# All 32 turning transfers issued by SyncE in a two-spectrum filter kernel

## The chip, the core and the metric

The kernel runs on one core of a Trainium2 chip. The core has five engines with queues of their own: TensorE (PE in the profile; PEld is its weight load), VectorE (DVE), ScalarE (ACT), GpSimd (POOL) and SyncE (SP). Sixteen DMA engines move data between memory and the on-chip buffer, and inside that buffer. A DMA is issued by one of the queues; the queue then goes on to its next instruction, and a semaphore tells of the landing.

The metric is the device time of one execution in microseconds, the median over several runs. All times below are in microseconds.

## The reference

One input x of 2048 rows by 1024 columns (bf16) goes through two spectral filters, A and B, and a gate mixes the two results row by row:

```python
X = jnp.fft.rfft2(x.astype(jnp.float32), axes=(-2, -1))
a = jnp.fft.irfft2(X * (A_w_r + 1j * A_w_i), s=(2048, 1024), axes=(-2, -1)).astype(jnp.bfloat16)
b = jnp.fft.irfft2(X * (B_w_r + 1j * B_w_i), s=(2048, 1024), axes=(-2, -1)).astype(jnp.bfloat16)
g = sigmoid((x * gate_w).sum(-1, keepdims=True))
return g * a + (1 - g) * b
```

The weights have 2048 rows by 513 columns. Both filters read the same x, so the forward transform is made once and the inverse transform twice.

## The kernel before

**How the work is tiled.** The 2048 rows are split as 128 times 16: a row is 16 times a partition number plus a remainder n2 from 0 to 15. Every transform is written as matrix products against constant matrices. The forward part goes through the rows in pairs of n2 (stage S1), then through the columns (stage D), then through the 16 remainders (stage S2). The spectrum lies in 16 slots on 128 partitions, in four groups `sq` of four slots.

**The products with the weights.** VectorE multiplies each pair of slots with the weights of A (b = 0) and of B (b = 1): `prod`, tiles of 128 x 2052.

**The inverse over the 16 remainders, and the turn.** `stage_iw` (for b = 0) and `stage_i1` (for b = 1) multiply the products with a small constant matrix on TensorE and leave two results of 128 x 1024 each, for j = 0 and 1, the two halves of the partitions. ScalarE or VectorE evicts each result from PSUM into a tile V in RING. There are seven such tiles (`"v": ("ring", 14)`, two cells each), used again and again. Then one DMA per tile, 256 KB, moves it from RING into TV so that partitions and remainders change places: this is the turning transfer, `dma("turn" ...)` or `dma("turnw" ...)`.

- A wide turn (`turnw`, from `stage_iw`, all 16 for b = 0) writes 8 partitions of TV, 16 rows of 1024 elements (2 KB) in each. Its access pattern is 8x16x1024.
- An ordinary turn (`turn`, from `stage_i1`, all 16 for b = 1) writes 16 partitions, 8 rows of 2 KB in each: 16x8x1024. It belongs to one half `th` of the remainders: th = 0 for n2 below 8, th = 1 for the others.

So there are 32 turns, 8 MB in all. In this text "(1,3,0) j=0" is the ordinary turn of b = 1, sq = 3, th = 0, first half of the partitions.

**The inverse over the rows, the columns, the folds.** For each remainder n2, stage S1 inverse multiplies turned data with the gated matrices FM (for A) and RM (for B). For n2 = 0 to 3 it is cut into an A part (`S1A`) and a B part (`S1B`); for the others it is one group (`S1H`). `S1A` needs all 16 wide turns. `S1B` and `S1H` need the ordinary turns of their half th as well. The result is evicted (G), multiplied with the constant DI (`Di2`, `Di`), evicted again (o), and folded by VectorE (u, e, y0, y1) into a row tile y, which SyncE stores (`dma("out" ...)`). The fold's tiles u and y lie in RING too, in cells which the V tiles used before.

**What sets the order.** The whole order is written out. `ORDER` is a table with the sequence of all nodes, `ENGS` gives the engine of each node where the node allows several (p TensorE, a ScalarE, d VectorE, g GpSimd, s SyncE), and `CELLS` gives each tile its place. `Plan.replay` reads the three, and `Sched` turns data dependences into semaphore waits. Every engine executes its nodes strictly in the order of the table. A DMA waits in its queue for what it needs, and what stands behind it in the same queue waits with it.

**The two queues of interest.** SyncE (SP) issues the loads of x, the constants F, DM, SK, RM and DI, eight ordinary turns and the nine stores. GpSimd (POOL) issues 44 weight loads, the 16 wide turns and eight ordinary ones (24 turns). The constant DI is read first by `Di2`. In the program it is loaded by

```python
cload("sp", DI, 0, "DI", 0, 2048, ["DI"], more=wk[1])
```

which waits for the weights of B (`more=wk[1]`), and its place among the turns is set by `ORDER`. All DMAs are issued by one line of the helper, L426 in the profile; evictions by ScalarE are L417, by VectorE L418, VectorE's two-operand instructions L395, matrix products L392.

## Time and profile before

| what | value |
|---|---|
| median of 3 runs | 123.09 (122.49 to 123.79) |
| profiled execution, its own time | 124.25 |
| its span, first to last instruction of the program | 122.4 |
| mean granted TensorE clock | 0.979 |
| busy: PE / DVE / ACT / POOL | 103.8 / 103.4 / 93.5 / 40.1 |
| turns issued by POOL / by SP | 24 / 8 |
| one turn's issue on POOL, mean; TV<-RING, issue to landing on POOL / SP, median | 0.577; 5.7 / 7.8 |
| DMA traffic, mean over the span | 228 GB/s |

How to read it: the span is cut into 40 slices of 3.06 each on the profile's page, and a digit is the busy share in tenths. The chain of waits is followed back from the last instruction. Durations of matrix products overlap, since the array is pipelined. An instruction's "idle before" is the time for which its engine had nothing to do ahead of it, with the releaser that the profile infers; where the named releaser had long been done or is not what the instruction reads, it was another, often a DMA.

The turns run from 51.6 on. Until 77 VectorE multiplies without a pause; then the last evictions and turns of b = 1 follow, and from 85.7 on the inverse over the rows.

### The profile page before, as it was taken

How to read it: one execution, taken by the hardware profiler on the slowest of the kernel's cores; microseconds unless marked ns; L12 is line 12 of the kernel's file. 1: busy time of each engine (PE TensorE's matmuls, PEld its weight loads, DVE VectorE, ACT ScalarE, POOL GpSimd, SP SyncE). 2: the span in 40 equal slices, each digit the busy share in tenths (PEclk: the TensorE clock that was granted, in tenths of full speed). 3: DMA queues.
4: the chain of work that ended last, by engine and by line, in shares of the span. 5: the costliest groups of instructions: out<-in, count | busy, mean ns of one | idle time of the engine just before them, and what ended most of it. 6: DMA issues, size and time to landing. Idle time of an engine off the chain costs nothing.

```text
span 122.4 us, 3773 instructions
## 1 busy us (share of the span) xinstructions
PE 103.8 (85%) x1652; PEld 71.6 (58%) x1652; DVE 103.4 (84%) x139; ACT 93.5 (76%) x106; POOL 40.1 (33%) x72
## 2 busy tenths in 40 slices
PE   6879968999999998999797977795999999993820
PEld 2258747797665753454254424342899999992500
DVE  0459999928889999999999999759586599999990
ACT  4098999277799789999798897623499999984930
POOL 0006599999994000163525323031500000000000
PEclk9999999999999999999999999999999999999587
DMA  4999999999999960047886677699999102148664
GB/s 81 395 422 414 402 354 251 329 348 318 334 284 343 314 171 3 5 99 169 227 215 182 174 196 220 174 244 247 269 262 237 44 5 102 70 193 327 253 261 171
DMA packets 10754, 27.86 MB, mean 228 GB/s; under 512 B 4049, under 2 KB 4049, under 8 KB 10482
## 3 DMA queue, kind: packets, MB, share of 16 engines
q0 software_dynamic: 6272, 14.73, 42.9%
q1 hardware_dynamic: 4320, 12.88, 30.6%
q8 instruction: 13, 0.21, 0.7%
q10 hardware_dynamic: 146, 0.02, 0.1%
q14 instruction: 3, 0.02, 0.1%
HBM read 15.01 MB, written 4.19 MB: 157 GB/s over the span
## 4 chain that ended last, share of the span: by engine, by line
DVE 54%; PE 21%; ACT 11%; issue 5%; DMA 5%; SPq 1%; DVEq 0%
DVE WAB L395 23%; PE PS L392 21%; DVE RING L395 14%; DVE TV L395 5%; DMA WAB<-in_A_x_dram 5%; ACT R L417 4%; DVE RING L418 4%; DVE R L395 4%; ACT RING L417 3%; ACT TV L417 3%; DVE TV L418 2%; DVE FM L395 1%; DVE WAB L418 1%; DVE R L418 1%; ACT WAB L417 1%
## 5 line engine op out<-in xcount | busy, mean ns | idle before, releaser
L417 ACT ACTIVATE RING<-PS 128x1024 bf16<-128x1024 f32 x38 | 37.0, 1023 | 13.4 <-PE PS L392 12.9
L395 DVE TENSOR_TENSOR RING<-WAB 128x1024 bf16<-128x1024 bf16 (+1 forms) x42 | 23.6, 612 | 7.6 <-DMA WAB<-in_A_x_dram 5.1
L426 POOL DMA_DIRECT2D TV<-RING x24 | 13.8, 577 | 36.0 <-ACT RING L417 31.4
L395 DVE TENSOR_TENSOR WAB<-R,WAB 128x2052 bf16<-128x2052 bf16 x20 | 23.8, 1226 | 0.1
L417 ACT ACTIVATE WAB<-PS 128x1024 bf16<-128x1024 f32 (+1 forms) x25 | 20.2, 970 | 2.7 <-DVE WAB L395 2.1
L392 PE MATMUL PS<-WAB,SK 64*32 64x512 bf16 (+1 forms) x512 | 20.5, 377 | 1.6 <-DVE RING L418 0.6
L417 ACT ACTIVATE R<-PS 128x1024 bf16<-128x1024 f32 (+1 forms) x20 | 17.6, 947 | 2.2 <-PE PS L392 2.2
L418 DVE CAST RING<-PS 128x1024 bf16<-128x1024 f32 x10 | 12.1, 1220 | 4.6 <-PE PS L392 4.6
L392 PEld LDWEIGHTS PS<-WAB,SK 64*32 64x32 bf16 (+1 forms) x512 | 9.4, 95 | 10.3 <-DVE WAB L395 2.0
L392 PE MATMUL PS<-DM,TV 128*128 128x256 bf16 x128 | 15.2, 274 | 0.1
L392 PE MATMUL PS<-FM,TV 128*128 128x128 bf16 x128 | 13.3, 220 | 2.2 <-ACT WAB L417 2.1
L392 PE MATMUL PS<-TV,RING 128*128 128x256 bf16 (+1 forms) x128 | 12.6, 253 | 2.8 <-DVE RING L395 1.4
L392 PEld LDWEIGHTS PS<-DM,TV 128*128 128x128 bf16 x128 | 13.5, 114 | 2.3 <-issue 1.0
L392 PEld LDWEIGHTS PS<-FM,TV 128*128 128x128 bf16 x128 | 12.5, 113 | 3.1 <-ACT WAB L417 2.4
L417 ACT ACTIVATE TV<-PS 128x1024 bf16<-128x1024 f32 x14 | 13.3, 1043 | 0.5 <-PE PS L392 0.5
L392 PEld LDWEIGHTS PS<-TV,RING 128*128 128x128 bf16 x128 | 10.2, 98 | 5.2 <-DVE RING L395 1.9
L392 PE MATMUL PS<-RM,TV 128*128 128x128 bf16 x128 | 13.1, 219 | 0.0
L392 PEld LDWEIGHTS PS<-RM,TV 128*128 128x128 bf16 x128 | 12.6, 114 | 0.0
L426 POOL DMA_DIRECT2D WAB<-in_A_w_r_dram x11 | 6.7, 612 | 11.4 <-DMA WAB<-in_A_x_dram 11.4
L392 PE MATMUL PS<-RING,SK 64*64 64x511 bf16 (+2 forms) x160 | 9.3, 340 | 0.8 <-ACT R L417 0.5
L395 DVE TENSOR_TENSOR TV<-R,WAB 128x2052 bf16<-128x2052 bf16 x8 | 9.6, 1226 | 0.4 <-DVE R L418 0.4
L392 PE MATMUL PS<-TV,SK 64*64 64x512 bf16 x128 | 8.5, 380 | 1.3 <-DVE WAB L395 0.9
(46 smaller groups left out, 117.2 us busy)
## 6 DMA issues: line engine op xcount, KB each, us to landing
TV<-RING POOLq DMA_DIRECT2D x24, 256.0 KB, 5.7
WAB<-in_A_x_dram SPq DMA_DIRECT2D x8, 512.0 KB, 7.8
out_dram<-RING SPq DMA_DIRECT2D x7, 512.0 KB, 2.9
TV<-RING SPq DMA_DIRECT2D x8, 256.0 KB, 7.8
WAB<-in_A_w_r_dram POOLq DMA_DIRECT2D x2, 513.0 KB, 8.8
WAB<-in_A_w_i_dram POOLq DMA_DIRECT2D x2, 513.0 KB, 8.1
WAB<-in_B_w_r_dram POOLq DMA_DIRECT2D x2, 513.0 KB, 7.7
WAB<-in_B_w_i_dram POOLq DMA_DIRECT2D x2, 513.0 KB, 9.9
```

What stands on the lines that cost most here:

```text
L392: return lambda e: e.matmul(o, l, r, start=start, stop=stop, skip_group_check=True)
L395: return lambda e: e.tensor_tensor(out=o, in0=a, in1=b, op=op)
L417: return [lambda e: e.activation(o, i, ACT.Copy)]
L418: return [lambda e: e.tensor_copy(o, i)]
L426: n = P.add(name, es, lambda e: [lambda q, d=d, s=s: q.dma_start(d, s) for d, s in pairs()], reads, writes, dma=kind, **kw)
```

## The change

All 32 turns are issued by SyncE. GpSimd keeps the weight loads and issues nothing after them. The table of order, the engines of all other nodes, and all places of tiles are the same. In the code two arguments change, and 24 letters g of `ENGS` become s:

```diff
 ENGS = (
...
-    "ppaddddddpaapaappppdaaddddappaapppppadpdpdddaappdaadppgggggggggggaapaaaasdddddpddaapaapddddddddddddddddddaappaagpaaggggg"
-    "gggggppaapaapaappaapppapaaddppgggggggppaddadpppdadpaddssssggggggsssssppppppppapdappddaapapapapapappppaaadddddddddddddppa"
+    "ppaddddddpaapaappppdaaddddappaapppppadpdpdddaappdaadppgggggggggggaapaaaasdddddpddaapaapddddddddddddddddddaappaaspaasssss"
+    "sssssppaapaapaappaapppapaaddppsssssssppaddadpppdadpaddsssssssssssssssppppppppapdappddaapapapapapappppaaadddddddddddddppa"
...
-            dma("turn", ("sp", "pool")[j], lambda j=j: [(AP(TV, (64 * j + sq) * pt + vat(b, 8 * th), [[4 * pt, 16], [(2048, 1024)[b], 8], [1, 1024]]),
+            dma("turn", "sp", lambda j=j: [(AP(TV, (64 * j + sq) * pt + vat(b, 8 * th), [[4 * pt, 16], [(2048, 1024)[b], 8], [1, 1024]]),
...
-            dma("turnw", "pool", lambda j=j: [(AP(TV, (64 * j + 32 * a + sq) * pt + b * 16384, [[4 * pt, 8], [1024, 16], [1, 1024]]),
+            dma("turnw", "sp", lambda j=j: [(AP(TV, (64 * j + 32 * a + sq) * pt + b * 16384, [[4 * pt, 8], [1024, 16], [1, 1024]]),
```

TensorE's, VectorE's and ScalarE's queues hold the same instructions in the same order as before. GpSimd's queue ends after the last weight load. What changes is SyncE's queue. Its beginning, from the last constants of the forward part on, was this before (RM is the matrix for B in the inverse over the rows; s_act and s_dve are the semaphores of ScalarE and VectorE, s_d and a number that of a DMA; xN counts equal rows in sequence):

```order
L426 DMA SK<-c_SK 128x1152
L426 DMA RM<-c_RM 128x2048 [waits s_d17,s_d18,s_d16,s_d19,s_d15,s_d20,s_d14,s_d21,s_d13,s_d22,s_d23]
L426 DMA TV<-RING 16x8x1024 [waits s_act]
L426 DMA TV<-RING 16x8x1024 x2
L426 DMA TV<-RING 16x8x1024 [waits s_act]
```

and it is this now:

```order
L426 DMA SK<-c_SK 128x1152
L426 DMA RM<-c_RM 128x2048 [waits s_d17,s_d18,s_d16,s_d19,s_d15,s_d20,s_d14,s_d21,s_d13,s_d22,s_d23]
L426 DMA TV<-RING 8x16x1024 [waits s_act] x7
L426 DMA TV<-RING 8x16x1024
L426 DMA TV<-RING 8x16x1024 [waits s_act]
L426 DMA TV<-RING 16x8x1024 [waits s_act]
L426 DMA TV<-RING 8x16x1024 [waits s_act]
L426 DMA TV<-RING 8x16x1024 x2
```

The wide turns (8x16x1024) now stand on SyncE's queue, behind RM, and each waits there for its own eviction. The second place is around the load of DI. Before, SyncE's queue had, behind the first four ordinary turns:

```order
L426 DMA TV<-RING 16x8x1024 [waits s_act]
L426 DMA DI<-c_DI 128x2048
L426 DMA TV<-RING 16x8x1024
L426 DMA TV<-RING 16x8x1024 [waits s_dve]
L426 DMA TV<-RING 16x8x1024 [waits s_act]
L426 DMA TV<-RING 16x8x1024 [waits s_dve]
```

and now, from the last wide turn on:

```order
L426 DMA TV<-RING 8x16x1024
L426 DMA TV<-RING 16x8x1024 [waits s_act]
L426 DMA TV<-RING 16x8x1024 x2
L426 DMA TV<-RING 16x8x1024 [waits s_act]
L426 DMA TV<-RING 16x8x1024
L426 DMA TV<-RING 16x8x1024 [waits s_dve] x3
L426 DMA TV<-RING 16x8x1024
L426 DMA TV<-RING 16x8x1024 [waits s_act]
L426 DMA DI<-c_DI 128x2048
L426 DMA TV<-RING 16x8x1024 x3
L426 DMA TV<-RING 16x8x1024 [waits s_dve]
```

Six turns that were GpSimd's now stand ahead of DI: (1,2,0) j=1, (1,3,0) j=1, and the four turns j=1 of th = 1, namely (1,0,1), (1,3,1), (1,1,1) and (1,2,1). The last of these waits for the last eviction but one of the whole stage. The four turns j=0 of th = 1 stay behind DI.

## The prediction

> **What bounds the kernel now.** I read the chain of waits first, from 84 us on, because the edit touches nothing before 51 and the turns' readers stand here.

> ```profile
> 83.86 1.98 PE PS L392 x64
> ...
> 86.94 5.57 PE PS L392 x80
> ...
> 92.53 1.02 ACT WAB L417
> 93.55 2.76 ACT R L417 x3
> 96.31 0.03 issue
> 96.34 0.76 DVE RING L395 x2
> ```

> Up to 92.5 TensorE carries it, after 96.3 VectorE, to the end. The timelines of PE and of VectorE show the two hand-overs:

> ```profile
> 85.72 2.30 PE L392 MATMUL PS<-FM,TV 128*128 128x128 bf16 x32
> 87.86 1.95 PE L392 MATMUL PS<-RM,TV 128*128 128x128 bf16 x32
> 89.69 2.80 PE L392 MATMUL PS<-DI,R 128*128 128x128 bf16 x32
> ```

> ```profile
> 93.19 0.76 DVE L395 TENSOR_TENSOR RING<-WAB 128x512 bf16<-128x512 bf16 x2
> 96.34 0.76 DVE L395 TENSOR_TENSOR RING<-WAB 128x512 bf16<-128x512 bf16 x2 [2.38 <-ACT R L417]
> ...
> 100.63 1.22 DVE L418 CAST WAB<-PS 128x1024 bf16<-128x1024 f32 x1
> ```

> S1A, S1B and Di2 of n2 = 0 to 3 follow each other on PE without a gap; the third group reads DI. VectorE stands idle for 2.38 ahead of the fold u of n2 = 0. The releaser named writes R, which this fold doesn't read. It reads o of n2 = 0, evicted by ScalarE at 93.55, and writes a RING tile that a V tile had: that of (1,1,1) j=1. Its turn's issue and its landing:

> ```profile
> 85.83 1.04 POOL L426 DMA_DIRECT2D TV<-RING  x2 [1.21 <-DVE RING L418]
> 87.17 0.53 POOL L426 DMA_DIRECT2D TV<-RING  x1 [0.29 <-ACT RING L417]
> ```

> ```profile
> TV<-RING POOLq DMA_DIRECT2D x1, 256.0 KB, 9.9
> ```

> The second of the pair starts at about 86.35 and lands 9.9 later, at 96.24, just ahead of 96.34. So VectorE's last stretch waits for the backlog of turns. From 77 to 97 that backlog keeps the DMA engines full (share 0.90), and two stages before they are not:

> ```profile
> 52.90:54.20 1.30, 1.30 (x28) 0.58 (x16) 1.30 (x2) 1.30 (x2) 0.74 (x2) 1.00 0.46 66
> 57.00:66.00 9.00, 7.46 (x192) 3.34 (x188) 8.97 (x9) 8.04 (x10) 3.58 (x7) 1.00 0.85 224
> 77.00:97.00 20.00, 17.88 (x414) 13.84 (x399) 13.41 (x17) 12.38 (x14) 3.17 (x6) 1.00 0.90 224
> ```

> (The last two columns are the DMA engines' share and GB/s.)

> **The change part by part.** *The issue itself.* GpSimd starts a turn 0.29 after the eviction (row 87.17: ScalarE's eviction ended at 86.88). SyncE needs 0.02:

> ```profile
> 76.12 1.03 ACT L417 ACTIVATE RING<-PS 128x1024 bf16<-128x1024 f32 x1
> ```

> ```profile
> 77.17 0.62 SPq L426 DMA_DIRECT2D TV<-RING  x1
> ```

> An issue takes 0.62 there against 0.53 to 0.60. Each turn is thus issued 0.27 sooner, if SP isn't held by a turn ahead; nothing that ends late reads that, so I cost it at nothing.

> *DI moves back.* This is the term that counts. SP's own timeline before:

> ```profile
> 77.17 3.67 SPq L426 DMA_DIRECT2D TV<-RING  x4
> 80.88 1.08 SPq L426 DMA_DIRECT2D DI<-c_DI  x1
> 82.01 5.63 SPq L426 DMA_DIRECT2D TV<-RING  x4
> ```

> ```profile
> DI<-c_DI SPq DMA_DIRECT2D x1, 512.0 KB, 8.7
> ```

> DI landed at 80.88 + 8.7 = 89.55, and Di2 began at 89.69: already no slack. Now SP must first issue (1,2,1) j=1, whose eviction on ScalarE ends at

> ```profile
> 85.86 1.02 ACT L417 ACTIVATE RING<-PS 128x1024 bf16<-128x1024 f32 x1 [2.26 <-PE PS L392]
> ```

> 86.88. With 0.02, the issue of 0.62 and 0.04 between two, DI is issued at 87.56, 6.7 later. Behind it in the queue wait the four turns j=0 of th = 1 (issued from 82.01 on before); ahead of it, in the DMA engines, what SP issued before. For their pace I take the landing of the turn at 77.17, which finds its queue empty (the second row is the one at 80.31), and packets while only SP's turns run (80.3 to 81.3):

> ```profile
> TV<-RING SPq DMA_DIRECT2D x1, 256.0 KB, 4.4
> ...
> TV<-RING SPq DMA_DIRECT2D x1, 256.0 KB, 7.1
> ```

> ```profile
> q1 hardware_dynamic: 123, 0.22, 105.8%
> ```

> 0.22 MB in 1 us is 1.2 for a turn of 0.262 MB; so 4.4 is 1.2 of transfer and 3.2 of fixed delay. The six turns of th = 0 start at 77.17 and finish one per 1.2 at best: landings 81.6, 82.8, 84.0, 85.2, 86.4, 87.6. The last is just ahead of S1B at 87.86, as it was before (SP's issue at 80.31, landed 7.1 later). If it is late, DI's own lateness covers it up to 4. Then (1,0,1) lands at 88.8; (1,3,1), issued at 85.56 behind VectorE's eviction below, at 90.0; (1,1,1) at 91.2; (1,2,1) at 92.4. DI is 0.524 MB into all partitions; the loads of x at the start, of the same size and shape, run at up to 422 GB/s:

> ```profile
> 84.32 1.22 DVE L418 CAST RING<-PS 128x1024 bf16<-128x1024 f32 x1
> ```

> ```profile
> GB/s 81 395 422 414 402 354 251 329 348 318 334 284 343 314 171 3 5 99 169 227 215 182 174 196 220 174 244 247 269 262 237 44 5 102 70 193 327 253 261 171
> ```

> so 1.28 more, and DI lands at 93.65. Di2 moves from 89.69 to 93.7: PE loses 4.0, and all that PE feeds moves by it, since it runs gapless there.

> *What the slack takes.* o of n2 = 0 then is evicted at 93.55 + 4.0 = 97.55 instead of 93.55, and VectorE's fold waits for that, no longer for the turn, which lands at 91.2 now. It starts at 97.6 against 96.34: +1.2 to +1.3. VectorE is busy without pause from there (from 98 on seven slices of 9 in its row of the page), so this goes to the end.

> ```profile
> DVE  0459999928889999999999999759586599999990
> ```

> The readers that I use below, from the timelines of PE and VectorE:

> ```profile
> 96.78 1.92 PE L392 MATMUL PS<-DI,R 128*128 128x256 bf16 x21
> 98.54 0.22 PE L392 MATMUL PS<-FM,TV 128*128 128x128 bf16 x1
> ```

> ```profile
> 99.42 1.29 DVE L395 TENSOR_TENSOR RING<-WAB 128x1024 bf16<-128x1024 bf16 x2
> ```

> Two smaller terms: the eviction of o for n2 = 7 at 100.63 waits for the last but one of four products, which end at 98.70 (96.78 + 1.92) 0.66 apart. It moves from 98.04 to 102.05, against 101.9 for the delayed VectorE: +0.2. And ScalarE, in its last stretch,

> ```profile
> 103.38 6.24 ACT L417 ACTIVATE WAB<-PS 128x1024 bf16<-128x1024 f32 x7
> 111.71 5.13 ACT L417 ACTIVATE WAB<-PS 128x1024 bf16<-128x1024 f32 x8 [2.09 <-DVE WAB L395]
> ```

> ended its stretch before the wait at 109.62; moved by 4.0 this is 113.6, past 111.71 + 1.4 = 113.1: +0.5. The last four turns land at 94.9, 96.1, 97.3, 98.5; their first reader, S1H of n2 = 13, moves from 98.54 to 102.5, and the row tile y of n2 = 2, which reuses the last one's cells at 99.42, to 100.8. Both are covered. Sum: 1.2 + 0.2 + 0.5 = **+1.9**.

> *The wide turns move to one hardware queue.* A wide turn keeps eight of the sixteen DMA engines busy: 0.46 in the first window above, where the first one flies nearly alone, and 0.85 where several of GpSimd's overlap. So GpSimd's turns spread over different eights. Where SP's would go no row shows, since SP issued none. If always to the same eight, each takes 16 packets of 2 KB per engine, one after another. Lower end: the store packets late in the run (120.3 to 121.3) give 100.8% of 16 us for 0.39 MB, 84 ns per 2 KB, so 1.34 per wide turn. Upper end: the row at 80.3 (105.8%, 0.22 MB) gives 158 ns, so 2.5.

> ```profile
> q1 hardware_dynamic: 204, 0.39, 100.8%
> ```

> ```profile
> 51.55 0.62 POOL L426 DMA_DIRECT2D TV<-RING  x1 [13.59 <-ACT RING L417]
> ```

> From 51.3 (this row less the 0.29) to 77.17, when the turns of th = 0 begin, 25.9 are there for 16 wide and two ordinary turns: 16 x 1.34 + 2 x 1.2 = 23.8. They just fit, up to 1.47 per wide turn; each 0.1 above costs 1.6. I take 1.4, nearest to the 84 ns: eight engines write eight partitions, while in the 158 ns row sixteen write at once. Then nothing is added. No eviction waits for a landing before either (ScalarE's RING row names PE alone), so a somewhat later V tile costs nothing.

> ```profile
> ACT RING L417 <- PE PS L392: 7.8, 7, 2.3
> ```

> [...]

> **The rivals.**

> *The eight engines fall behind.* If a wide turn takes over 1.47, the backlog reaches the turns of th = 0, S1B, and DI behind them in the same queue. For it speaks the pace of GpSimd's own wide turns: in 57 to 66, 224 GB/s at 0.85 of sixteen engines is 125 ns per 2 KB, 2.0 for a wide turn on eight. Against: the first window says that their beginnings are what is slow. At 1.75 the price is 16 x 0.28 = 4.5 on top of the 1.9, so 129.5; at 2.0 8.5, so 133.5; at 2.5 some 142.

> *Not slower: VectorE's idle time takes all.* The place is the 2.38 ahead of 96.34: it ends with a turn's landing, which comes 5 sooner now, so the first part of any delay of PE is free. By the sum above the end moves by 1 for each 1 of DI: 1.9 at 93.65, 1.2 at 92.95, nothing at 91.75; that is the point from which it decides, and the time there is 123.1. It needs the three turns ahead of DI to take 0.6 instead of 1.2 each, or a shorter fixed delay. Were the queue empty, DI would land at 87.56 + 3.2 + 1.28 = 92.0, so 123.3. With the 2.9 that SP's stores of the same size take it would be 90.5, so 121.8.

> ```profile
> out_dram<-RING SPq DMA_DIRECT2D x7, 512.0 KB, 2.9
> ```

> For it: the price hangs on 1 to 2 us of DI, from rows that other traffic disturbed. Against: 105.8% at 0.22 MB, and 224 GB/s from 77 to 97, are the slow pace.

> That the change does nothing can't be: DI's place in the queue is fixed by the code.

> **How the numbers follow.** The span is 122.4 in an execution of 124.25, 1.85 outside it; that execution lies 1.16 over the median of 123.09. I add the 1.9 to the median: 125.0. A measurement of this kernel tells about 1% from no change, here 1.2.

> The forecast, DI late by 3.3 to 5.5 and 1.2 to 3.4 at the end (124.3 to 126.5): 0.45. The backlog on eight engines, 126.5 and above: 0.27. The idle time takes it: 0.28, of which 0.23 within 1% and 0.05 faster, since only the landing at 90.5 gives more than 1.2 back. So faster 0.05, same 0.23, slower 0.72. The range leaves out the quick end of the last case (0.1) and wide turns above 1.84 (0.1): 123.6 to 131.

> **What would show it.** Right: DI's issue at 87.5 on SP, its landing at 93 to 94, PE idle for about 4 ahead of the first product that reads DI, VectorE's pause ahead of the fold on n2 = 0 ended by ScalarE's eviction, and the turns of th = 0 landed by 88. The wide turns landing 4 to 7 after their issue, without growing, shows that eight engines keep up. Wrong: S1A or S1B (readers of TV) waiting for turns beyond 88, which is the backlog; or DI landed by 91.8 and the last stretch starting at 96.3 or sooner. SP's issues stretching past 1, as DI's 1.08 did, would add to the delay.

## The result, and the profile after

The changed kernel takes 128.01 us (median of 4 runs, 127.85 to 129.0) against 123.4 for the kernel before beside it (122.49 to 123.79): a ratio of 1.042, with an interval of 1.034 to 1.051. It is slower, as forecast, and by more: 4.6 where 1.9 was expected. The profiled execution took 129.0 with a span of 127.2; that of before took 124.25 and 122.4. So the two traces lie 4.75 apart, and it is these 4.75 that the rows below account for.

First the page of the changed kernel: TensorE, VectorE, the granted clock and the DMA engines in 40 slices of 3.18 us, and the group that reads DI.

```profile
PE   6789969999999979998979778869129999999710
...
DVE  0469999758799999999999997685303899999991
...
PEclk9999999999999999999999999999965899999995
DMA  4999999999999970255575566999995000438574
...
L392 PE MATMUL PS<-DI,R 128*128 128x128 bf16 (+1 forms) x64 | 8.1, 306 | 4.9 <-DMA DI<-c_DI 4.9
...
TV<-RING SPq DMA_DIRECT2D x32, 256.0 KB, 5.4
```

There is one hole, in slices 29 to 31 (from 89.0 to 98.6): TensorE falls to 1 and 2, VectorE to 3, 0 and 3, and from the second of these slices on the clock is at 6, 5 and 8 tenths. Elsewhere the clock stands at 9, but for the last slice, behind TensorE's last product. The DMA row is at 5 to 7 from 54 to 79, where the wide turns fly, so they leave part of the sixteen DMA engines idle, and at 9 from 79.5 to 95.

The chain of waits of the changed kernel, from 84 on, goes through that hole:

```profile
86.74 1.42 SPq L426
88.16 0.04 issue
88.20 6.16 DMA DI<-c_DI
94.36 0.14 issue
94.49 10.94 PE PS L392 x120
105.43 0.02 issue
105.45 1.22 DVE WAB L418
```

An issue of a turn on SyncE, DI's own load, and then TensorE for 10.94 without a pause; VectorE takes over only at 105.45. Before, it had taken over at 96.34. SyncE's timeline of the changed kernel shows DI where the order had put it, ahead of the four turns j=0 of th = 1, and TensorE's timeline what it cost:

```profile
85.97 2.18 SPq L426 DMA_DIRECT2D TV<-RING  x2
88.20 0.59 SPq L426 DMA_DIRECT2D DI<-c_DI  x1
88.83 0.54 SPq L426 DMA_DIRECT2D TV<-RING  x1
```

```profile
87.69 1.95 PE L392 MATMUL PS<-RM,TV 128*128 128x128 bf16 x32
94.49 5.28 PE L392 MATMUL PS<-DI,R 128*128 128x128 bf16 x32 [4.85 <-DMA DI<-c_DI]
```

The four groups that read DI start at 94.49 after 4.85 of idle time (before: 89.69, with none), and then they take 5.28 instead of 2.80. The second is a loss that the prediction doesn't have. VectorE's timeline shows how both reach the folds:

```profile
95.97 1.23 DVE L418 CAST WAB<-PS 128x1024 bf16<-128x1024 f32 x1 [5.96 <-PE PS L392]
98.53 1.22 DVE L418 CAST WAB<-PS 128x1024 bf16<-128x1024 f32 x1 [1.33 <-PE PS L392]
99.86 0.76 DVE L395 TENSOR_TENSOR RING<-WAB 128x512 bf16<-128x512 bf16 x2
100.87 0.76 DVE L395 TENSOR_TENSOR RING<-WAB 128x512 bf16<-128x512 bf16 x2 [0.25 <-ACT WAB L417]
101.54 2.50 DVE L395 TENSOR_TENSOR WAB<-RING,WAB 128x1024 bf16<-128x1024 bf16 x4
...
105.45 1.22 DVE L418 CAST WAB<-PS 128x1024 bf16<-128x1024 f32 x1 [0.21 <-PE PS L392]
```

The fold on n2 = 0, which started at 96.34, starts at 100.87: 4.53 later. The eviction for n2 = 7 waits another 0.21 and starts at 105.45 instead of 100.63, 4.82 later. From there to the end the distance between the two traces stays (4.75 in the profiled times).

Why the four groups took 5.28 is in the windows of the changed kernel, cut at the steps in which its clock changes (3.41 us each: in before the granted clock falls to 0.5 at 113.79, is back at 1.0 at 117.21 and falls again at 120.62; the columns are length, busy time of PE, PEld, DVE, ACT and POOL, the granted clock, the DMA share and GB/s):

```profile
89.60:93.00 3.40, 0.04 (x1) 0.00 (x0) 0.41 (x1) 1.59 (x2) 0.00 (x0) 1.00 1.05 277
93.00:96.40 3.40, 1.91 (x13) 1.57 (x14) 0.43 (x1) 0.00 (x0) 0.00 (x0) 0.50 1.06 207
96.40:99.80 3.40, 3.40 (x24) 2.79 (x23) 2.02 (x2) 1.02 (x1) 0.00 (x0) 0.50 0.16 33
99.80:103.20 3.40, 3.40 (x63) 3.40 (x62) 3.10 (x7) 3.39 (x4) 0.00 (x0) 0.99 0.00 0
```

A step in which TensorE did next to nothing is followed by two at half clock. In the third row TensorE is busy all the time and gets through 24 products; in the fourth it gets through 63.

### The profile page after: what moved, and what is told of

It is laid out like the page before. It is cut to its first block, busy times and chain, and to the rows that moved or that the text cites. A ratio compares the mean times of both kernels' runs of the same rounds, so it can differ in the third digit from the quotient of the medians.

```text
span 127.2 us, 3773 instructions
## 1 busy us (share of the span) xinstructions
PE 105.1 (83%) x1652; PEld 72.8 (57%) x1652; DVE 103.4 (81%) x139; ACT 93.4 (73%) x106; POOL 26.4 (21%) x48
## 4 chain that ended last, share of the span: by engine, by line
DVE 49%; PE 24%; DMA 9%; ACT 8%; issue 5%; SPq 2%; DVEq 0%
PE PS L392 24%; DVE WAB L395 20%; DVE RING L395 12%; DMA DI<-c_DI 5%; DVE TV L395 5%; DMA WAB<-in_A_x_dram 4%; DVE RING L418 4%; DVE R L395 4%; ACT RING L417 3%; ACT TV L417 3%; DVE TV L418 2%; SPq L426 2%; ACT R L417 2%; DVE FM L395 1%; DVE WAB L418 1%
## 5 line engine op out<-in xcount | busy, mean ns | idle before, releaser
L417 ACT ACTIVATE RING<-PS 128x1024 bf16<-128x1024 f32 x38 | 37.0, 1023 | 13.4 <-PE PS L392 12.9
L395 DVE TENSOR_TENSOR RING<-WAB 128x1024 bf16<-128x1024 bf16 (+1 forms) x42 | 23.6, 613 | 5.4 <-DMA WAB<-in_A_x_dram 4.9
L417 ACT ACTIVATE WAB<-PS 128x1024 bf16<-128x1024 f32 (+1 forms) x25 | 19.9, 1014 | 7.6 <-PE PS L392 7.6
L395 DVE TENSOR_TENSOR WAB<-R,WAB 128x2052 bf16<-128x2052 bf16 x20 | 23.8, 1228 | 0.1
L392 PE MATMUL PS<-WAB,SK 64*32 64x512 bf16 (+1 forms) x512 | 20.5, 377 | 1.6 <-DVE RING L418 0.6
L417 ACT ACTIVATE R<-PS 128x1024 bf16<-128x1024 f32 (+1 forms) x20 | 17.7, 946 | 2.1 <-PE PS L392 2.1
L418 DVE CAST RING<-PS 128x1024 bf16<-128x1024 f32 x10 | 12.1, 1219 | 4.6 <-PE PS L392 4.6
L392 PE MATMUL PS<-DM,TV 128*128 128x256 bf16 x128 | 15.2, 274 | 0.1
L392 PEld LDWEIGHTS PS<-WAB,SK 64*32 64x32 bf16 (+1 forms) x512 | 9.4, 95 | 10.2 <-DVE WAB L395 2.0
L392 PE MATMUL PS<-TV,RING 128*128 128x256 bf16 (+1 forms) x128 | 12.6, 253 | 2.8 <-DVE RING L395 1.3
L392 PEld LDWEIGHTS PS<-DM,TV 128*128 128x128 bf16 x128 | 13.5, 114 | 2.3 <-issue 1.0
L417 ACT ACTIVATE TV<-PS 128x1024 bf16<-128x1024 f32 x14 | 13.3, 1043 | 0.4 <-PE PS L392 0.4
L392 PE MATMUL PS<-FM,TV 128*128 128x128 bf16 x128 | 13.5, 221 | 0.1
L392 PEld LDWEIGHTS PS<-TV,RING 128*128 128x128 bf16 x128 | 10.2, 98 | 5.3 <-DVE RING L395 1.9
L392 PE MATMUL PS<-RM,TV 128*128 128x128 bf16 x128 | 13.2, 220 | 0.0
L392 PEld LDWEIGHTS PS<-FM,TV 128*128 128x128 bf16 x128 | 12.6, 115 | 0.9 <-DVE RING L418 0.4
L392 PEld LDWEIGHTS PS<-RM,TV 128*128 128x128 bf16 x128 | 12.6, 114 | 0.0
L392 PE MATMUL PS<-DI,R 128*128 128x128 bf16 (+1 forms) x64 | 8.1, 306 | 4.9 <-DMA DI<-c_DI 4.9
L392 PEld LDWEIGHTS PS<-DI,R 128*128 128x128 bf16 x64 | 6.6, 123 | 6.1 <-issue 5.0
L392 PE MATMUL PS<-RING,SK 64*64 64x511 bf16 (+2 forms) x160 | 9.3, 340 | 0.7 <-ACT R L417 0.5
L395 DVE TENSOR_TENSOR TV<-R,WAB 128x2052 bf16<-128x2052 bf16 x8 | 9.6, 1224 | 0.4 <-DVE R L418 0.4
L418 DVE CAST WAB<-PS 128x1024 bf16<-128x1024 f32 x3 | 3.7, 1224 | 7.5 <-PE PS L392 7.5
## 6 DMA issues: line engine op xcount, KB each, us to landing
TV<-RING SPq DMA_DIRECT2D x32, 256.0 KB, 5.4
WAB<-in_A_x_dram SPq DMA_DIRECT2D x8, 512.0 KB, 7.6
out_dram<-RING SPq DMA_DIRECT2D x7, 512.0 KB, 2.7
```

The source lines that it names most:

```text
L392: return lambda e: e.matmul(o, l, r, start=start, stop=stop, skip_group_check=True)
L395: return lambda e: e.tensor_tensor(out=o, in0=a, in1=b, op=op)
L417: return [lambda e: e.activation(o, i, ACT.Copy)]
L418: return [lambda e: e.tensor_copy(o, i)]
```

## The experiments

The first question was what the loss is made of: DI's late load (the forecast), or the wide turns on one hardware queue (the first rival), or something in the queue itself. Once DI was found to be most of it, the next were whether the rest is the granted clock, and whether VectorE's idle time takes the first part of a delay as the prediction had it. The table gives what the traces show; "fold chain" is the start of VectorE's four folds at 97.01 in before (101.54 in after), which stands for the end. Landings and starts are those of one execution of each kernel, so the medians follow them to about 1 only: with the wide turns alone on SyncE the chain starts 0.76 sooner than in before, at the same median.

| kernel | DI landed | products on DI start, take | granted clock during them | fold chain | median us | ratio to before |
|---|---|---|---|---|---|---|
| before | 89.55 | 89.69, 2.80 | 1.0 | 97.01 | 123.4 | |
| after | 94.36 | 94.49, 5.28 | 0.5 | 101.54 | 128.01 | 1.042 (1.034 to 1.051) |
| after, DI early | 49.7 | 89.24, 2.80 | 1.0 | 94.10 | 121.99 | 0.990 (0.987 to 0.993) |
| before, DI early | 50.0 | 89.48, 2.80 | 1.0 | 95.33 | 122.0 | 0.989 (0.985 to 0.993) |
| before, wide turns on SyncE | 90.3 | 90.45, 2.80 | 1.0 | 96.25 | 123.4 | 1.003 (1.000 to 1.005) |
| before, ordinary turns on SyncE | 93.58 | 93.72, 4.24 | 0.5 | 99.73 | 127.47 | 1.035 (1.031 to 1.039) |
| before, DI behind SyncE's last turn | 98.18 | 98.32, 4.48 | 0.5 | 104.85 | 131.52 | 1.069 (1.060 to 1.078) |
| after, 20 fillers | 94.75 | 94.80, 2.81 | 1.0 | 99.67 | 126.42 | 1.026 (1.020 to 1.033) |
| after, DI behind two | 91.5 | 91.62, 4.46 | 0.5 | 98.14 | 125.35 | 1.021 (1.015 to 1.027) |
| after, DI behind three | | | | | 126.88 | 1.029 (1.024 to 1.034) |
| after, DI behind two, 9 fillers | 92.65 | 92.70, 2.81 | 1.0 | 97.57 | 124.11 | 1.006 (1.002 to 1.010) |

**DI taken out of the way.** The changed kernel, with DI's load put right behind RM's, ahead of the first turn. In the string that sets the order, its node moves:

```diff
-...7d7e7h7f5k6566...        ...8e788k7o842r7m768i82...
+...7d7e7h7f2r5k6566...      ...8e788k7o847m768i82...
```

> The changed kernel with one node moved: the load of DI stands right behind RM on SyncE's queue, ahead of the first turn, so it lands near 51. All 32 turns stay on SyncE in the same order. Theory A (DI's late landing and TensorE's half clock after the idle time are the whole loss): the loss of about 4.6 goes; VectorE's last stretch no longer waits for a turn and starts up to 2.4 sooner than in the kernel before, so 121.5 (121 to 123). Theory B (one hardware queue for all turns, the wide ones on eight engines, is what costs): still 126 to 128. A mixture shows as a time between 123.5 and 126.

TensorE's timeline and VectorE's of this kernel:

```profile
89.24 2.80 PE L392 MATMUL PS<-DI,R 128*128 128x128 bf16 x32
```

```profile
90.10 2.54 DVE L418 CAST WAB<-PS 128x1024 bf16<-128x1024 f32 x2 [0.33 <-PE PS L392]
92.75 1.43 DVE L395 TENSOR_TENSOR RING<-WAB 128x512 bf16<-128x512 bf16 x4
94.10 2.49 DVE L395 TENSOR_TENSOR WAB<-RING,WAB 128x1024 bf16<-128x1024 bf16 x4
```

No idle time ahead of the products, none ahead of the folds, the granted clock at 1.0 in the products (0.993 in the mean of the span), and 121.99: all of the loss is gone and 1% more, with all 32 turns still on SyncE. What stays of the change once DI is away costs nothing. The load itself is issued at 46.27 and lands 3.4 later, where it had taken 8.7 in before and 6.2 in after.

**The same move without the change.** The kernel before, turns on two queues, with the same move of DI's node (the diff above).

> The kernel before with the load of DI moved right behind RM, ahead of the first turn; the turns keep their two queues. Theory A (the place of DI decides, the queue of the turns hardly): DI's 1.3 to 2 leaves the backlog of the last turns, the turn of (1,1,1) j=1 lands some 1.5 sooner, VectorE's fold starts near 95, and the time is 121.8 to 122.4, the same as the 121.99 of the changed kernel with DI early. Theory B (SyncE's queue itself brings something): 122.8 to 123.4.

122.0 and a ratio of 0.989, the same as the last one. Its VectorE still waits for a turn ahead of the fold on n2 = 0,

```profile
94.66 0.76 DVE L395 TENSOR_TENSOR RING<-WAB 128x512 bf16<-128x512 bf16 x2 [0.91 <-DMA TV<-RING]
```

but for 0.91 instead of 2.38. So with DI out of the way it makes no measurable difference which engine issues the turns, and both versions beat both kernels by about 1%.

**The wide turns alone.** The kernel before, with only the 16 wide turns on SyncE; the ordinary ones stay on two queues, and DI behind the same turns as before.

```diff
-            dma("turnw", "pool", lambda j=j: ...
+            dma("turnw", "sp", lambda j=j: ...
```

> The kernel before with the 16 wide turns alone moved to SyncE; the ordinary turns keep their two queues, and DI its place. Theory A: wide turns take about 1.4 each on eight engines and keep up, nothing else changes: 123.4, within 1 of the kernel before. Theory B (the eight engines fall behind): the turns of th = 0 land past 88, and the time is 126 or more.

123.4 and a ratio of 1.003. The backlog of the first rival doesn't form: DI landed at 90.3, and TensorE's timeline has the products on it without idle time ahead of them.

```profile
90.45 2.80 PE L392 MATMUL PS<-DI,R 128*128 128x128 bf16 x32
```

**The ordinary turns alone.** The counterpart: the kernel before, with GpSimd's eight ordinary turns on SyncE; the wide ones stay on GpSimd.

```diff
-            dma("turn", ("sp", "pool")[j], lambda j=j: ...
+            dma("turn", "sp", lambda j=j: ...
```

> The kernel before with the eight ordinary turns of GpSimd alone moved to SyncE; the 16 wide turns stay on GpSimd. DI then stands behind the same six turns as in the changed kernel. Theory A: DI lands near 94.4, TensorE idles 4.8, and the time is that of the changed kernel, 127.3 to 129. Theory B (the wide turns have a share in the loss): 124 to 126.

127.47, within 0.6 of the whole change. TensorE's timeline, and the windows at its clock's steps:

```profile
93.72 4.24 PE L392 MATMUL PS<-DI,R 128*128 128x128 bf16 x32 [4.06 <-DMA DI<-c_DI]
```

```profile
88.00:91.40 3.40, 1.65 (x30) 1.49 (x27) 1.23 (x1) 2.86 (x3) 0.00 (x0) 1.00 1.04 255
91.40:94.80 3.40, 1.08 (x13) 1.05 (x14) 0.23 (x1) 0.00 (x0) 0.00 (x0) 1.00 1.06 248
94.80:98.20 3.40, 3.40 (x26) 2.83 (x25) 2.38 (x3) 1.23 (x2) 0.00 (x0) 0.51 0.49 97
```

DI landed at 93.58, and TensorE lost 4.06: nearly the forecast's 93.65 and 4.0. That is luck in part: the turn ahead of DI landed at 91.62, 0.8 sooner than the 92.4 of the working, and DI's own transfer then took 1.96 instead of 1.28. The part of the change that costs is the six turns that come to stand ahead of DI, and the clock's loss comes with it.

**DI late, no turn moved.** The kernel before, with DI's node behind SyncE's last turn of the stage:

```diff
-...842r7m768i82978q...
+...847m768i822r978q...
```

> The kernel before with the load of DI moved behind SyncE's last turn, where it is issued near 87.7 as in the changed kernel; all turns keep their queues. Theory A: DI lands behind the backlog near 96 to 98, TensorE idles 6 to 8 ahead of the first product with DI, its clock falls to half, and the time is 128 to 133. Theory B: DI's place costs little, 123 to 125.

131.52. DI, issued at 88.32, landed at 98.18, and TensorE lost 7.87:

```profile
98.32 4.48 PE L392 MATMUL PS<-DI,R 128*128 128x128 bf16 x32 [7.87 <-DMA DI<-c_DI]
```

The clock's row of this kernel's page (slices of 3.25):

```profile
PEclk9999999999999999999999999999955899999998
```

A late DI by itself makes this kind of loss, with the turns on their two old queues, and the half clock comes with it here too.

**The clock kept up.** The changed kernel with 20 filler products (128x128 by 128x512, of DM with itself) ahead of the products on DI for n2 = 1. They write that group's PSUM tile, which the group overwrites, and bridge the time in which TensorE waits for DI.

```diff
+    P.key = ("fill", 1)
+    pe("fill", [512] * 20, lambda t=FILL[0]: [mm(psl(t, 0, [[1, 512]]), ap(DM, 0, [[1, 128]]), ap(DM, 0, [[1, 512]]), True, True) for _ in range(20)], ["DM"], [(FILL[0],)], alloc=[FILL[0]])
```

> The changed kernel with 20 more products of 128x128 by 128x512 on TensorE, from DM into the PSUM tile that the first product with DI overwrites, between S1B and that product: about 4.3 of work in the 4.85 of idle time. If the idle time makes the clock fall: it stays at 1.0, the four groups with DI take 2.8 again instead of 5.3, and the time is 2 to 2.6 below the changed kernel's 128, near 125.5. If the clock falls for another reason (the time since the start, or the work before), the time stays at 128.

TensorE's timeline of this kernel (19 of the 20 have a record), and the clock's row of its page:

```profile
89.84 4.26 PE L392 MATMUL PS<-DM 128*128 128x512 bf16 x19
94.80 2.81 PE L392 MATMUL PS<-DI,R 128*128 128x128 bf16 x32 [0.69 <-DMA DI<-c_DI]
```

```profile
PEclk9999999999999999999999999999999999999995
```

DI landed at 94.75, no sooner than in the changed kernel (94.36), yet the products take 2.81 again and the median is 126.42 (four runs, 125.76 to 127.68), 1.6 less. That is short of the 2 to 2.6 expected; DI landed 0.4 later here, so at the same landing it would be some 2.0. Work that nobody reads made the kernel faster; that part of the loss was the clock. What remains, 3.2 over the kernel before beside it (123.23), is close to what the prediction's slope of 1 for 1 gives for this landing: 94.75 - 91.75 = 3.0.

**A smaller delay.** The changed kernel with DI's node moved forward, so that only two of the four turns j=1 of th = 1 stand ahead of it:

```diff
-...8e788k7o842r7m...
+...8e788k2r7o847m...
```

> The changed kernel with DI's load two places further ahead: behind (1,3,1) j=1, ahead of (1,1,1) and (1,2,1) j=1. It is issued near 86.1 and lands near 92.1; TensorE idles 2.5 ahead of the first product with DI. Theory A (idle time of VectorE takes the first 2 of it, and an idle time under 3.4 leaves the clock at 1.0): 123.3 to 124. Rival (any idle time costs in full, or the clock falls at 2.5 too): 125.5 or more.

This missed: 125.35. DI landed at about 91.5, so by the slope nothing should be lost, and the idle time is under one step of the clock. But:

```profile
91.62 4.46 PE L392 MATMUL PS<-DI,R 128*128 128x128 bf16 x32 [2.31 <-DMA DI<-c_DI]
```

```profile
88.30:91.70 3.40, 1.09 (x21) 0.96 (x19) 1.23 (x1) 2.57 (x3) 0.00 (x0) 1.00 1.05 266
91.70:95.10 3.40, 3.40 (x22) 2.68 (x22) 1.23 (x1) 0.79 (x1) 0.00 (x0) 0.51 1.06 219
95.10:98.50 3.40, 3.40 (x59) 3.32 (x57) 2.94 (x6) 2.62 (x4) 0.00 (x0) 0.99 0.40 81
```

2.31 of idle time, all of it in one step, was enough to halve the clock for the whole next step. With DI behind three of the four (the string then reads ...8k7o2r847m...) this was expected:

> The changed kernel with DI's load one place further ahead: behind (1,1,1) j=1, ahead of (1,2,1) j=1 alone. It is issued near 86.7 and lands near 93.2; TensorE idles 3.6. If the clock stays at 1.0: 124.3 to 125.2. If it falls (the granted clock changes in steps of 3.41, and 3.6 of idle time holds less than two of them): 126 to 127.5.

and the median was 126.88 (ratio 1.029, 1.024 to 1.034), in the range that had been given for a clock that falls.

**A smaller delay, the clock kept up.** The kernel with DI behind two turns, with nine of the fillers.

> The changed kernel with DI's load behind (1,3,1) j=1, as in the run that gave 125.35, and 9 products of 128x128 by 128x512 (about 1.9 of work) on TensorE between S1B and the first product with DI, which idled 2.3 there and then ran its four groups in 4.46 instead of 2.80 at half clock. New theory (the granted clock is set by how busy TensorE was in the last 3.41, not by a whole 3.41 of idle time): the clock stays at 1.0, the groups take 2.8, and the time is 123.4 to 124.2. Rival (the late DI itself costs it, through evictions or VectorE): 125 or more again.

124.11, against 125.35 without them. Its timeline, and the window that answers to the one with 1.09:

```profile
89.90 2.11 PE L392 MATMUL PS<-DM 128*128 128x512 bf16 x9
92.70 2.81 PE L392 MATMUL PS<-DI,R 128*128 128x128 bf16 x32 [0.70 <-DMA DI<-c_DI]
```

```profile
88.40:91.80 3.40, 3.40 (x39) 2.29 (x36) 1.23 (x1) 2.85 (x3) 0.00 (x0) 1.00 1.04 235
```

The clock stays up, and 1.2 of the 2.0 that the smaller delay had cost comes back, though DI happened to land 1.2 later (92.65). The rest, 0.9 over 123.18, is again what the slope gives: 92.65 - 91.75 = 0.9.

## Why the prediction was right on the sign and short on the size

**DI behind six turns: right.** It was issued behind (1,2,1) j=1, and its landing is what TensorE waited for, once, for 4.85. Moving DI alone removes the loss (121.99), delaying DI alone makes one (131.52), and moving only the turns that come to stand ahead of it makes nearly all of it (127.47).

**The turns' pace: right at the end, by errors that cancel.** The four turns ahead of DI landed at 88.75, 90.09, 91.25 and 92.40, where 88.8, 90.0, 91.2 and 92.4 stood; the last of th = 0 landed at 87.53 (87.6). The products S1B, which read those, started at 87.69 without waiting. But the first of the six of th = 0 landed at 80.51, where 81.6 stood, and the six then took 1.40 each and not 1.2; the late start of the working made up for its quick pace. The four behind them kept 1.2.

**DI's own transfer: mis-sized.** It was to land 1.28 after the turn ahead of it, and took 1.96. In the kernel with DI behind all of SyncE's turns it took 0.99 after the turn ahead; that nothing stood behind it there, and four turns did in the changed kernel, would fit, but wasn't tried by itself. In all seven traces of the table in which turns stand behind DI in its queue it took 1.96 to 2.16, and the kernel before is one of them: DI landed at 89.55, the turn issued ahead of it at 80.31 + 7.1 = 87.4. Both numbers stood in the prediction; with their 2.1 it would have had DI land at 94.5. The 1.28 came from the loads of x at the start. The issue came at 88.20 instead of 87.56 because the issue ahead of it took 1.42 instead of 0.62; that cost nothing by itself, since DI landed behind the turns and not behind its own issue. In sum DI landed 0.71 later than forecast, and TensorE started at 94.49, 0.8 after the 93.7 of the working.

**The step that failed: "Di2 moves by 4.0, and all that PE feeds moves by it".** It took the products behind the gap at their old speed. They ran at half clock: 5.28 instead of 2.80, so 2.48 more in the profiled execution. With that the fold on n2 = 0 comes out: 97.6 forecast, plus 0.8, plus 2.48, is 100.9, and the trace has 100.87. In the medians the clock's share, by the fillers, is 1.6 (128.01 to 126.42), or some 2.0 at the same landing. It has no fixed size: in the four tabled kernels at half clock the products lost 1.4, 1.7, 1.7 and 2.5. The row with the half clock stood in the profile of before, at another place, and was not read as a price of idle time. The windows of before at its clock's steps, in the kernel's last stretch:

```profile
110.40:113.80 3.40, 1.28 (x19) 0.93 (x16) 3.37 (x7) 2.09 (x3) 0.00 (x0) 1.00 0.65 267
113.80:117.20 3.40, 2.94 (x14) 1.47 (x12) 3.40 (x9) 3.00 (x7) 0.00 (x0) 0.50 0.77 308
```

TensorE busy for 1.28 of 3.4, and the next 3.4 at 0.50. A stall of TensorE by 2.3 that falls into one step leaves it less busy than that (1.09, in the kernel with DI behind two) and has this price on it; so has a gap of 4.06, the size of the forecast's own 4.0, in the kernel with the ordinary turns on SyncE.

**What the slack takes: right, at full clock.** VectorE's idle time ahead of the fold did absorb the first part. Where the clock stayed up, the medians rose by 3.2 and 0.9, where DI's landing less 91.75 is 3.0 and 0.9. In the traces the fold chain moved from 97.01 to 99.67 and 97.57: one for one with the landings of 94.75 and 92.65, but counted from 92.1. So the slope is borne out, and its zero only to some 0.4. "Nothing at 91.75" was still wrong for the time: at 91.5 the kernel lost 2.0, because TensorE's own gap of 2.3 halved the clock there (4.46 instead of 2.80), which VectorE's idle time can't take.

**The two smaller terms.** +0.2 for the eviction of n2 = 7 showed as the idle 0.21 ahead of 105.45. +0.5 for ScalarE's last stretch didn't show: between 105.45 and the end VectorE lost no more against before.

**The first rival: fell.** With the wide turns alone on SyncE the time is the kernel's own (1.003). In the changed kernel they landed one per 1.39 where several were queued (55.33 to 66.43 in eight steps), under the 1.47 from which a backlog was to build; 1.4 had been taken. The windows of the changed kernel, one with only wide turns flying and the one that stood at 0.85 in before:

```profile
52.50:56.00 3.50, 3.34 (x64) 1.77 (x54) 3.50 (x4) 3.46 (x4) 0.00 (x0) 1.00 0.52 149
57.00:66.00 9.00, 7.46 (x192) 3.36 (x188) 8.97 (x9) 8.03 (x10) 0.00 (x0) 1.00 0.61 210
```

A share of 0.52, about what eight of the sixteen engines make (0.52 x 16 = 8.3), with 149 GB/s where GpSimd's first wide turn had 66 at 0.46: quicker at nearly the same share. Each wide turn's completion came as nine updates of its semaphore in the changed kernel (for the first turn, issued at 51.12, one at 52.27 and eight from 54.87 to 55.33), where each of GpSimd's had sixteen in before (for the first, issued at 51.55, from 53.21 to 55.71). Which engines SyncE's wide turns went to, these traces don't show. The measured time of 128.0 lies in the span of times that this rival had been given, but not for its reason.

**The second rival: fell for the change as it is**, since DI landed at 94.36. It holds for a DI that comes back to 90.3, as in the kernel with the wide turns alone.

The forecast's own range of 124.3 to 126.5 would have held the kernel at full clock (126.42 with the fillers); the time of 128.0 is inside 123.6 to 131 only through the reach to the first rival. That it lies there is luck: the time came from DI and the clock, and not from wide turns.

## What to carry to other kernels

When DMAs move to another in-order queue, list what then stands behind them there: a constant's load of one instruction was the whole cost here, and the queue of the 32 turns none. Load a constant early, where the DMA engines have little to do (46 us, landed in 3.4), and not among the transfers that it competes with (5.5 to 9.9); that alone made this kernel 1% faster. Where a stall leaves most of a clock step idle (TensorE busy for 1.1 or less of 3.4 here), price it at its length plus what the products behind it lose at half clock (1.4 to 2.5 here), and look for a step at half clock in the profile of before to see how short a stall is enough.

## What the runs showed of the hardware that was not expected

The same load of DI, issued at 85.65 and 85.66 behind the same turns in two kernels, landed at about 91.5 and at 92.65. The fillers, which run from 89.9 on, don't make this difference: an ordinary turn ahead of DI, issued at 76.69 and 76.70, already landed 3.4 and 5.2 after its issue. What does make it was not found.
